# Two MLP layers planned task by task by the list scheduler, with the last attention pair's sums and products placed inside the first MLP

## The chip, the cores and the metric

The kernel runs on one core of one Trainium2 chip. The time is the device time of one execution in microseconds (us); the kernel before takes 679.59 us, the median of three runs (677.91, 679.59 and 680.23).

The core has a matrix engine (TensorE, PE in the rows), a vector engine (VectorE, DVE), a scalar engine (ScalarE, ACT), a general engine (GpSimd, called Pool here, POOL in the rows) and a queue that issues the loads and stores (SyncE, SP). Each engine does its own instructions in program order; between engines there are semaphores.

## The reference

Queries are averaged in twos, attention runs over 16 heads (2 batches of 8) of 1152 keys, and the 1152 x 512 result goes through two MLPs of 512 -> 2048 -> 512, the first with a leaky rectifier and the second with h times sigmoid(h). The weights arrive as 64-bit floats.

```python
def _attn_ref(q, k, v):                     # q, k, v: (2, 8, 1152, 64)
    q_pool = q.reshape(B, H, S // 2, 2, D).mean(axis=3)
    scores = scale * np.matmul(q_pool, k.transpose(0, 1, 3, 2))
    attn = np.exp(scores - np.max(scores, axis=-1, keepdims=True))
    attn = attn / (np.sum(attn, axis=-1, keepdims=True) + 1e-09)
    return np.matmul(attn, v)
...
x = attn_out.transpose(0, 2, 1, 3).reshape(B * S, H * D)     # 1152 x 512
h = x @ w_in;  x = np.maximum(0.01 * h, h) @ w_out           # first MLP
h = x @ w2_in; x = (h * (1.0 / (1.0 + np.exp(-h)))) @ w2_out # second MLP
```

## The kernel before

**Numbers in two parts.** TensorE multiplies operands of type fp32r. To keep precision every operand of the MLPs is held as a high part and a low part, and each product is three matmuls: high x high, low x high, high x low. So the MLPs' input is `xh` and `xl`, the weights are `w0h`/`w0l` (into the 2048) and `w1h`/`w1l` (out of them), and the values between are `gh` and `gl`.

**Attention.** Two heads make a pair; there are eight pairs. Their work is planned by `Plan`, a list scheduler that runs while the program is built: each task has an engine, an estimated length (`weight`), a due time, tasks that it comes after, and tokens or ring buffers that it takes and gives. Whenever an engine of the plan is free, the ready task with the earliest due time is written into the program. A pair's `pv` matmuls (L669) leave their sums in PSUM; ScalarE copies them to `pvs` (L683) in two halves. The sums of the exponentials come from `psum` matmuls with a tile of ones; for the last pair that is `sums_last`: TensorE L743 (two halves, two heads each), ScalarE L751 (to `r`), VectorE's reciprocals L757. Then `finish` multiplies (L766, VectorE), copies to `xh` (L769, ScalarE) and subtracts into `xl` (L770, VectorE). The last pair is the fourth 128-row slice of the second batch's columns, 576 to 1151.

**MLPs.** The 2048 inner columns are cut into four blocks of 512 (a block has four groups `f` of 128), the 1152 tokens into a narrow part of 512 and a wide part of 640 (two chunks of 320). A unit is (layer, block, part): 16 in all. `layer_in(u, f)` gives one PSUM tile `ph`: 12 matmuls of 512 columns, or 24 of 320. Then come the activation and the split: in the first MLP ScalarE twice (`gh`, `a`) and Pool `gl = a - gh` (L955); in the second ScalarE's sigmoid `t` (L952), VectorE's product `a` = h x t (L953), ScalarE's copy `gh` (L954), Pool's L955. `layer_out_t` (first MLP, `po`, L968) and `layer_out` (second, `pf`, L996) multiply the g tiles with the outgoing weights and add into an SBUF sum (L982 on VectorE). After the first MLP's last block ScalarE copies the sum to `xh` (L984) and Pool subtracts into `xl` (L985). `ph`, `po` and `pf` share four PSUM tiles; `t` and `a` have two buffers each.

**Weights.** They come in 64 pieces of 128 x 512 (four for each of a block's two matrices). A piece is loaded by SyncE (`raw`, three buffers), converted to 32 bits in five steps (ScalarE L131, then VectorE L135, L139, L143, L148, into `wt`, four buffers), and split (ScalarE L166 for the high part, Pool L170 for the low). Eight pieces are converted during attention, 56 in the MLPs.

**The order around the change.** Attention's plan ends before the MLPs begin. In `mlps` the order is written by hand: `phase_order` mixes the `layer_in` groups of a unit with the `layer_out` groups of the unit before, and at each `layer_in` group one piece is split, the next is converted with all its steps in one go, and one is loaded; only after that does `layer_in` write its own instructions (from the fourth unit on; the first two go by the tables `moe0` and `moe1`):

```python
        for x, u, i in order:
            if x is layer_in and ph > 2:
                weights.split()
                weights.convert()
                weights.load()
            x(u, i)
```

Of the kernel before, what the change touches and what calls it, by code (L numbers as in the profile page):

```python
# [19 lines left out]
def pooled_attention_two_mlps(  # L20
# [20 lines left out]
    with tc.manual_schedule():  # L41
        attention(tc, q, k, v, xh, xl, weights)
        mlps(tc, xh, xl, weights, out)
# [21 lines left out]
    weights_due=1.0,  # L65
    conv=8,
    split=4,
    wt=4,
    moe0=(0, 0, 0, 2),
    moe1=(2, 0, 1, 1),  # L70
# [216 lines left out]
def attention(ctx, tc, q, k, v, xh, xl, weights):  # L287
# [44 lines left out]
    ones = const.tile([128, D], F32, name="ones")  # L332
    tiny = const.tile([128, 1], F32, name="tiny")
# [317 lines left out]
    def sum_up(p, t, j, after, order, due):  # L651
        on_dve = (p, t, j) in dve_adds

        def go():
            e = nc.vector if on_dve else nc.gpsimd
            if t == 1:
                acc[p, j] = sm_p.tile([128, SQ], F32, tag="acc", name="acc", bufs=4)
            e.tensor_tensor(out=acc[p, j], in0=e_t[p, j, 0] if t == 1 else acc[p, j], in1=e_t[p, j, t], op=ALU.add)  # L658
# [18 lines left out]
    def evac_pv(p, after, due):  # L677
        made = []
        for c in range(2):
            def go(c=c):  # L680
                if c == 0:
                    pvs[p] = sm_p.tile([128, 2, C], F32, tag="pvs", name="pvs", bufs=1)
                nc.scalar.activation(out=pvs[p][:, c, :], in_=vps.pop((p, c))[:, 0:C], func=ACTF.Copy)  # L683
# [6 lines left out]
    def sums(p, after, due):  # L690
# [28 lines left out]
        def up2(j):  # L719
            if j == 0:  # L720
                rec[p] = sm_p.tile([128, 2, C], F32, tag="r", name="r", bufs=1)
# [15 lines left out]
    def sums_last(p, after, due):  # L737
        made = []
        for c in range(2):
            def pe(c=c):  # L740
                box["psum", c] = bank("psum")
                for j in range(2):
                    nc.tensor.matmul(  # L743
                        out=box["psum", c][0][own[j], 0:C], lhsT=ones, rhs=acc[p, j][:, c * C:(c + 1) * C], start=True, stop=True
                    )

            def act(c=c):
                ps, i = box.pop(("psum", c))
                if c == 0:
                    rec[p] = sm_p.tile([128, 2, C], F32, tag="r", name="r", bufs=1)  # L750
                nc.scalar.activation(out=rec[p][:, c, :], in_=ps[:, 0:C], func=ACTF.Identity, bias=tiny)  # L751
                banks.append(i)

            x = add("PE", 0.6, due, pe, after=after, take=("bank",))
            x = add("ACT", 0.5, due, act, after=[x], order=made, give=("bank",), take=() if c else ("r",))
            made.append(
                add("DVE", 1.95, due, lambda c=c: nc.vector.reciprocal(out=rec[p][:, c, :], in_=rec[p][:, c, :]), after=[x])  # L757
            )
        return made
# [36 lines left out]
    for p in range(NP):  # L796
# [62 lines left out]
        else:  # L859
            finish(p, sums_last(p, ends, at(1.0)) + values, at(1.0))  # L860
# [38 lines left out]
    attention.plan = plan  # L899
# [3 lines left out]
def mlps(ctx, tc, xh, xl, weights, out):  # L903
# [3 lines left out]
    FB, NBLK = weights.FB, weights.NBLK  # L907
    for key in ((0, 1), (1, 0), (1, 1)):
# [7 lines left out]


    groups = ((0, 1, 512), (512, 2, 320))
    g_t = {}
# [5 lines left out]
    def layer_in(u, f):  # L925
        layer, blk, g = u
        _, nch, n = groups[g]
        wh, wl = weights.tiles[layer * NBLK + blk, 0]
        fs = slice(f * 128, (f + 1) * 128)
        ps = ps_p.tile([128, 2, 512], F32, tag="p", name="ph")  # L930
        for kk in range(KDM):
            for wt, m in ((wh, xh), (wh, xl), (wl, xh)):
                for c in range(nch):
                    nc.tensor.matmul(  # L934
                        out=ps[:, c, 0:n],
                        lhsT=wt[:, kk, fs],
                        rhs=m[:, kk, chunk(g, c)],
                        start=(kk == 0 and wt is wh and m is xh),
                        stop=(kk == KDM - 1 and wt is wl),
                    )  # L940
        h = ps[:, 0:nch, 0:n]
        t = t_p.tile([128, 640], F32, tag="t", name="t")
        a = t_p.tile([128, 640], F32, tag="a", name="a")
        t, a = (x[:, 0:nch * n] for x in (t, a))
        t3, a3 = (x.rearrange("p (c n) -> p c n", n=n) for x in (t, a))
        gh, gl = (g_p.tile([128, 640], F32R, tag=f"g{part}{f}", name=f"g{part}") for part in "hl")
        if layer == 0:
            gh3 = gh[:, 0:nch * n].rearrange("p (c n) -> p c n", n=n)
            nc.scalar.activation(out=gh3, in_=h, func=ACTF.Prelu, alpha=0.01)
            nc.scalar.activation(out=a3, in_=h, func=ACTF.Prelu, alpha=0.01)  # L950
        else:
            nc.scalar.activation(out=t3, in_=h, func=ACTF.Sigmoid)  # L952
            nc.vector.tensor_tensor(out=a3, in0=h, in1=t3, op=ALU.mult)  # L953
            nc.scalar.activation(out=gh[:, 0:nch * n], in_=a, func=ACTF.Copy)  # L954
        nc.gpsimd.tensor_tensor(out=gl[:, 0:nch * n], in0=a, in1=gh[:, 0:nch * n], op=ALU.subtract)  # L955
        g_t[u, f] = (gh, gl)

    def layer_out_t(u, m):
        _, blk, g = u
        t0, nch, n = groups[g]  # L960
        oh, ol = weights.tiles[blk, 1]
        ms = slice(m * 128, (m + 1) * 128)
# [122 lines left out]
```

## Time and profile before

| | us |
|---|---|
| median of three runs | 679.59 |
| the profiled execution | 679.8 |
| its span, first to last instruction | 678.0 |
| TensorE busy (matmuls) | 654.2 (97%) |
| VectorE busy | 452.3 (67%) |
| Pool busy | 379.6 (56%) |
| ScalarE busy | 320.7 (47%) |
| moved by DMA | 59.71 MB, 88 GB/s on the mean |

An engine's busy time is the sum of its instructions' times in the profiled execution, and its share is taken of the span. Matmuls are pipelined, so that a busy share of TensorE near 100% does not tell how fast it goes: starts of instructions and the granted clock tell that. The DMA engines have little to do (their busy share is some 30% of the span).

### The profile page before, as it was taken

Reading aid. Unit: us, or ns where it says so; the run is one execution under the profiler, and the core shown is the slowest. Engines: PE = TensorE matmul, PEld = TensorE weight load, DVE = VectorE, ACT = ScalarE, POOL = GpSimd, SP = SyncE. Lnnn points to the kernel's source line nnn. Section 1 sums busy time; section 2 is a strip of 40 time slices with the busy share of each in tenths; the row PEclk is TensorE's granted clock in tenths of the full one; section 3 lists DMA queues with packets and bytes.
Section 4 is the critical chain, followed back from the end, with each engine's and each line's share of the span. In section 5 each row is a group of like instructions: output and inputs, shape, how many; then the busy total and the mean of one; then the engine's idle time right before and its main releaser. Section 6 shows DMA issues by size and latency. Waiting matters only on the chain.

```text
span 678.0 us, 10325 instructions
## 1 busy us (share of the span) xinstructions
PE 654.2 (97%) x3741; PEld 530.3 (78%) x3741; DVE 452.3 (67%) x698; ACT 320.7 (47%) x694; POOL 379.6 (56%) x294
## 2 busy tenths in 40 slices
PE   6899999999999999999999999999989999999997
PEld 4566667666666666989989989989867898888986
DVE  6776768587888867496667557476756677886222
ACT  5446566585766565555434234235344444334120
POOL 7566978878797830765445445365544354445120
PEclk9899999999999999999999999999989999999999
DMA  5535151536455220033223123012122222210012
GB/s 142 148 81 155 37 141 37 141 91 198 113 157 151 50 64 19 31 125 94 94 94 100 66 94 111 35 63 94 63 93 82 74 94 93 92 66 1 0 47 93
DMA packets 41898, 59.71 MB, mean 88 GB/s; under 512 B 15325, under 2 KB 24569, under 8 KB 41849
## 3 DMA queue, kind: packets, MB, share of 16 engines
q1 hardware_dynamic: 41848, 59.07, 29.9%
q8 instruction: 29, 0.48, 0.3%
q14 instruction: 21, 0.16, 0.1%
HBM read 49.81 MB, written 2.42 MB: 77 GB/s over the span
## 4 chain that ended last, share of the span: by engine, by line
PE 77%; DVE 12%; ACT 4%; DMA 3%; issue 2%; POOL 0%; SPq 0%; ACTq 0%; DVEq 0%
PE ph L934 24%; PE po L968 13%; PE pf L996 12%; PE pss L637 10%; PE pv L669 10%; PE pmx L583 4%; DVE mx L587 3%; PE prep L434 2%; DVE wt L139 2%; DVE wt L135 2%; DVE wt L143 1%; DMA d<-sum 1%; DVE a L953 1%; ACT wt L131 1%; DVE ql L491 1%
## 5 line engine op out<-in xcount | busy, mean ns | idle before, releaser
L955 POOL TENSOR_TENSOR gl<-a,gh 128x512 fp32r<-128x512 f32 (+1 forms) x64 | 95.1, 1488 | 163.4 <-ACT gh L954 107.5
L658 POOL TENSOR_TENSOR acc<-acc,e 128x576 f32<-128x576 f32 x98 | 140.1, 1451 | 29.0 <-ACT e L641 26.6
L641 ACT ACTIVATE e<-pss 128x288 f32<-128x288 f32 x288 | 101.4, 411 | 79.9 <-PE pss L637 73.0
L587 DVE TENSOR_REDUCE mx<-pmx 128x1 f32<-128x384 f32 x216 | 110.7, 550 | 34.4 <-PE pmx L583 29.2
L934 PE MATMUL ph<-xh,w0h 128*128 128x320 f32 (+1 forms) x384 | 109.1, 339 | 5.1 <-DVE a L953 4.5
L934 PE MATMUL ph<-xl,w0h 128*128 128x320 f32 (+1 forms) x384 | 108.9, 338 | 0.0
L934 PE MATMUL ph<-xh,w0l 128*128 128x320 f32 (+1 forms) x384 | 108.8, 338 | 0.0
L135 DVE TENSOR_SCALAR wt<-wt 128x512 f32<-128x512 f32 x56 | 44.6, 796 | 77.3 <-ACT wt L131 68.6
L637 PE MATMUL pss<-qh,k 128*128 128x288 f32 x288 | 87.8, 321 | 3.1 <-DVE mx L587 3.0
L669 PE MATMUL pv<-e,vnat 128*64 128x288 f32 x576 | 86.5, 422 | 0.0
L637 PE MATMUL pss<-ql,ka 128*128 128x288 f32 x288 | 81.2, 298 | 1.6 <-DMA ql<-mn 1.6
L934 PEld LDWEIGHTS ph<-xh,w0h 128*128 128x128 f32 x384 | 67.9, 189 | 13.1 <-DVE a L953 6.0
L637 PEld LDWEIGHTS pss<-qh,k 128*128 128x128 f32 x288 | 54.6, 190 | 24.9 <-DVE mx L587 10.3
L934 PEld LDWEIGHTS ph<-xh,w0l 128*128 128x128 f32 x384 | 67.5, 189 | 5.1
L934 PEld LDWEIGHTS ph<-xl,w0h 128*128 128x128 f32 x384 | 67.3, 189 | 4.6
L583 PE MATMUL pmx<-k,qh 128*128 128x384 f32 x192 | 65.4, 386 | 2.2 <-ACT e L641 1.0
L954 ACT ACTIVATE gh<-a 128x512 fp32r<-128x512 f32 (+1 forms) x32 | 22.0, 686 | 95.0 <-DVE a L953 95.0
L170 POOL TENSOR_TENSOR w1l<-wt,w1h 128x512 fp32r<-128x512 f32 x32 | 44.0, 1381 | 39.8 <-ACT w1h L166 39.8
L669 PEld LDWEIGHTS pv<-e,vnat 128*64 128x64 f32 x576 | 35.4, 137 | 28.9 <-issue 13.5
L996 PE MATMUL pf<-w1h,gh 128*128 128x512 f32 x144 | 56.5, 392 | 0.4 <-DVE a L953 0.3
L996 PE MATMUL pf<-w1h,gl 128*128 128x512 f32 x144 | 56.2, 390 | 0.6 <-POOL gl L955 0.6
L637 PEld LDWEIGHTS pss<-ql,ka 128*128 128x128 f32 x288 | 54.7, 190 | 2.0 <-issue 2.0
(82 smaller groups left out, 1137.7 us busy)
## 6 DMA issues: line engine op xcount, KB each, us to landing
wraw<-in_moe_w_in_dram SPq DMA_DIRECT2D x32, 512.0 KB, 3.8
wraw<-in_moe_w_out_dram SPq DMA_DIRECT2D x32, 512.0 KB, 3.3
vnat<-in_v_dram SPq DMA_DIRECT2D x8, 576.0 KB, 5.7
qnat<-in_q_dram SPq DMA_DIRECT2D x16, 256.0 KB, 4.7
knat<-in_k_dram SPq DMA_DIRECT2D x7, 576.0 KB, 5.4
ka<-k SPq DMA_DIRECT2D x16, 160.0 KB, 2.6
out_dram<-acc SPq DMA_DIRECT2D x9, 256.0 KB, 2.0
ka<-k SPq DMA_DIRECT2D x16, 128.0 KB, 2.5
```

The costliest lines, as they stand in the source:

```text
L135: nc.vector.tensor_scalar(out=tf, in0=tf, scalar1=2.0, scalar2=W_TOP, op0=ALU.max, op1=ALU.min)
L170: self.nc.gpsimd.tensor_tensor(out=lo, in0=tf, in1=hi, op=ALU.subtract)
L583: nc.tensor.matmul(out=ps[:, 0:KC], lhsT=QH[p, j][:, t * 128:(t + 1) * 128], rhs=K2[p, j][:, ks], start=True, stop=True)
L587: nc.vector.tensor_reduce(out=mx[p][:, n:n + 1], in_=ps[:, 0:KC], op=ALU.max, axis=AX.X)
L637: nc.tensor.matmul(out=ps[:, 0:C], lhsT=lhsT[:, ks], rhs=rhs[:, cs], start=not last, stop=last)
L641: nc.scalar.activation(out=e_t[p, j, t][:, cs], in_=ps[:, 0:C], func=ACTF.Exp, scale=scale)
L658: e.tensor_tensor(out=acc[p, j], in0=e_t[p, j, 0] if t == 1 else acc[p, j], in1=e_t[p, j, t], op=ALU.add)
L669: nc.tensor.matmul(out=vps[p, c][own[j], 0:C], lhsT=vnat[p][:, j, t, :], rhs=e_t[p, j, t][:, c * C:(c + 1) * C], start=(t == 0), stop=(t = ...
L934: nc.tensor.matmul(out=ps[:, c, 0:n], lhsT=wt[:, kk, fs], rhs=m[:, kk, chunk(g, c)], start=(kk == 0 and wt is wh and m is xh), stop=(kk == ...
L955: nc.gpsimd.tensor_tensor(out=gl[:, 0:nch * n], in0=a, in1=gh[:, 0:nch * n], op=ALU.subtract)
L968: nc.tensor.matmul(out=ps[:, c, 0:n], lhsT=wt[:, f, ms], rhs=x[:, c * n:(c + 1) * n], start=(f == 0 and wt is oh and x is gh), stop=(f == ...
L996: nc.tensor.matmul(out=ps[:, 0, :], lhsT=x[:, ts], rhs=wt[:, f, :], start=(f == 0 and x is gh and wt is oh), stop=(f == FB - 1 and x is gl),)
```

## The change

`sums_last` and its `finish` leave the attention's plan. A function `end` returns their steps instead: one step for TensorE (the four `psum` matmuls into one PSUM tile of the MLPs), one readout on ScalarE, and for each of two halves of 288 columns a reciprocal, a product, a copy to `xh` and a subtraction into `xl`. `pvs`, `r`, `acc`, `ones` and `tiny` move to a pool that lives through the MLPs.

`mlps` makes a `Plan` of its own. TensorE's groups get due times by adding up their estimated lengths in the order of `phase_order`, which is kept. Each group is four tasks (one for each `kk` or `f`), and each activation, product, copy, subtraction and sum is one task, due 3 us after its group's due time. A weight piece's load, five conversion steps and two split steps are tasks of their own, due `ahead` = 12 us before the piece's block is first used, plus 0.7 us for each piece in it. The pair's end is due at 2.5 us. Buffers are rings in the plan, as many as before. `moe0` and `moe1` go.

```diff
+    end=2.5,
+    ahead=12.0,
-    moe0=(0, 0, 0, 2),
-    moe1=(2, 0, 1, 1),
...
-    def sums_last(p, after, due):
+    def end(ps_p):
...
+        def pe():
+            box["end"] = ps_p.tile([128, 2, 512], F32, tag="p", name="psum")
+            for c in range(2):
                 for j in range(2):
...
+        def act():
+            rec[p] = end_p.tile([128, 2, C], F32, tag="r", name="r")
+            nc.scalar.activation(out=rec[p], in_=box["end"][:, :, 0:C], func=ACTF.Identity, bias=tiny)
...
-        else:
-            finish(p, sums_last(p, ends, at(1.0)) + values, at(1.0))
...
+    plan = Plan()
+    add = plan.add
+    for name, n in (("p", 4), ("t", 2), ("a", 2), ("raw", 3), ("wt", P["wt"])):
+        plan.ring(name, n)
+    for f in range(FB):
+        plan.ring(("g", f), 2)
...
+    for x in order:
+        kind, (layer, blk, g), i = x
+        due[x] = now
+        now += 3 * FB * (0.227 if g == 0 or (kind == "out" and layer == 1) else 0.292)
...
+    def piece_due(n):
+        blk, kind, i = pieces[n]
+        return first[blk, kind] - P["ahead"] + 0.7 * i
...
+                weigh = (("ACT", 0.66), ("DVE", 0.8), ("DVE", 1.1), ("DVE", 0.75), ("DVE", 0.75))
+                for m, (step, (eng, w)) in enumerate(zip(weights.convert_steps(), weigh)):
+                    x = [add(
+                        eng, w, d, step, after=x, order=[conv] if m == 0 and conv else [],
+                        take=(("wt", n),) if m == 0 else (), give=(("raw", n),) if m == 4 else (),
+                    )]
...
+            hi = add("ACT", 0.62, d, high, after=x, order=[hi] if hi else [])
+            lo = add("POOL", 1.45, d, low, after=[hi], give=(("wt", n),))
...
+            b = add(
+                "DVE", 0.83 if wide else 0.69, d,
+                lambda: nc.vector.tensor_tensor(out=three(tile("a")), in0=h(), in1=three(box["t", x]), op=ALU.mult),
+                after=[b], take=(("a", x),), give=(("p", x), ("t", x)),
+            )
...
+        t = add("PE", 1.2, P["end"], pe, take=(("p", "end"),), begin=P["end"])
+        t = add("ACT", 0.65, P["end"], act, after=[t], give=(("p", "end"),))
+        made = []
+        for c in range(2):
+            y = t
+            for m, (eng, w) in enumerate((("DVE", 1.93), ("DVE", 0.45), ("ACT", 0.45), ("DVE", 0.45))):
+                y = add(eng, w, P["end"], steps[c][m], after=[y])
```

Three places show what moves. A row here is one instruction in program order: line, operation, tile written <- tiles read, shape; the number behind a name tells its buffers apart, and the two programs number theirs differently.

The first is VectorE, and beside it ScalarE, early in the second MLP, at the second wide `ph` group of its first block, the one whose product is `a_5495` before and `a_5507` in the changed kernel. L953 and L1088 are the product. VectorE before:

```order
L135 TENSOR_SCALAR wt_5461<-wt_5461 128x512
L139 TENSOR_SCALAR wt_5461<-wt_5461 128x512
L143 SCALAR_TENSOR_TENSOR wt_5461<-wraw_5360,wt_5461 128x512
L148 SCALAR_TENSOR_TENSOR wt_5461<-wraw_5360,wt_5461 128x512
L953 TENSOR_TENSOR a_5495<-ph_5469,t_5494 128x640
L135 TENSOR_SCALAR wt_5518<-wt_5518 128x512
```

VectorE in the changed kernel:

```order
L135 TENSOR_SCALAR wt_5473<-wt_5473 128x512
L139 TENSOR_SCALAR wt_5473<-wt_5473 128x512
L143 SCALAR_TENSOR_TENSOR wt_5473<-wraw_5354,wt_5473 128x512
L1088 TENSOR_TENSOR a_5507<-ph_5453,t_5498 128x640
L148 SCALAR_TENSOR_TENSOR wt_5473<-wraw_5354,wt_5473 128x512
L135 TENSOR_SCALAR wt_5540<-wt_5540 128x512
L139 TENSOR_SCALAR wt_5540<-wt_5540 128x512
L1088 TENSOR_TENSOR a_5560<-ph_5516,t_5555 128x640
```

ScalarE before, at the same product (L952 sigmoid, L954 `gh`, L166 high part of a piece, L131 first step of the next):

```order
L954 ACTIVATE gh_5453<-a_5452 128x640
L166 ACTIVATE w0h_5383<-wt_5418 128x512
L131 ACTIVATE wt_5461<-wraw_5360 128x512
L952 ACTIVATE t_5494<-ph_5469 128x640
L954 ACTIVATE gh_5496<-a_5495 128x640
```

ScalarE in the changed kernel (L1084 sigmoid, L1093 `gh`):

```order
L131 ACTIVATE wt_5473<-wraw_5354 128x512
L1093 ACTIVATE gh_5482<-a_5471 128x640
L1084 ACTIVATE t_5498<-ph_5453 128x640
L1093 ACTIVATE gh_5513<-a_5507 128x640
L1179 ACTIVATE acc1_3466<-pf_5494 128x512
L166 ACTIVATE w1h_5408<-wt_5473 128x512
L131 ACTIVATE wt_5540<-wraw_5403 128x512
```

Before, each product follows a whole piece; in the changed kernel it follows three steps of one piece, and the next product the last step of it and two of the next. ScalarE's L131 for the piece ahead of this product stood behind the `gh` of the product before; in the changed kernel it stands ahead of that `gh`.

The second place is Pool where the first MLP's last wide unit turns into the second's input. Before, the four `xl` stand together:

```order
L170 TENSOR_TENSOR w1l_5135<-wt_5180,w1h_5134 128x512
L955 TENSOR_TENSOR gl_5235<-a_5233,gh_5234 128x512
L985 TENSOR_TENSOR xl_59<-acc1_3477,xh_58 128x640 x4
L170 TENSOR_TENSOR w1l_5135<-wt_5211,w1h_5134 128x512
L955 TENSOR_TENSOR gl_5378<-a_5376,gh_5377 128x512
```

In the changed kernel (L1149 is `xl`, L1099 `gl`):

```order
L1099 TENSOR_TENSOR gl_5248<-a_5238,gh_5247 128x512
L170 TENSOR_TENSOR w0l_5190<-wt_5196,w0h_5189 128x512
L1149 TENSOR_TENSOR xl_59<-acc1_3466,xh_58 128x640
L170 TENSOR_TENSOR w0l_5190<-wt_5250,w0h_5189 128x512
L1149 TENSOR_TENSOR xl_59<-acc1_3466,xh_58 128x640 x2
L170 TENSOR_TENSOR w0l_5190<-wt_5302,w0h_5189 128x512
L1149 TENSOR_TENSOR xl_59<-acc1_3466,xh_58 128x640
L170 TENSOR_TENSOR w1l_5409<-wt_5356,w1h_5408 128x512
```

Two weight splits stand among the four `xl` there. On VectorE the sums that they need (L1138 in the changed kernel) have conversion steps among them likewise, L148 and L135 ahead of the fourth.

The third place is TensorE where the MLPs begin. Before, the last pair's `psum` matmuls stand ahead of the first `ph` group:

```order
L743 MATMUL psum_3431<-acc_3238,ones_95 64x288
L743 MATMUL psum_3431<-acc_3248,ones_95 64x288
L743 MATMUL psum_3437<-acc_3238,ones_95 64x288
L743 MATMUL psum_3437<-acc_3248,ones_95 64x288
L934 MATMUL ph_3488<-xh_58,w0h_2050 128x512
```

In the changed kernel they stand behind the twelve matmuls of that group, of which the last three are shown:

```order
L1046 MATMUL ph_3467<-xh_58,w0h_2053 128x512
L1046 MATMUL ph_3467<-xl_59,w0h_2053 128x512
L1046 MATMUL ph_3467<-xh_58,w0l_2054 128x512
L747 MATMUL psum_3490<-acc_3241,ones_98 64x288
L747 MATMUL psum_3490<-acc_3251,ones_98 64x288
L747 MATMUL psum_3490<-acc_3241,ones_98 64x288
L747 MATMUL psum_3490<-acc_3251,ones_98 64x288
L1046 MATMUL ph_3502<-xh_58,w0h_2053 128x512
```

The second `ph` group follows them. Nothing else moves on TensorE, and nothing on SyncE's queue.

## Rows read from the trace of the kernel before

**Rows 1.** Windows view, us: PE, PEld, DVE, ACT, POOL busy (instructions), clock, DMA share, GB/s.

```profile
457.40:536.00 78.60, 72.71 (x374) 62.94 (x373) 51.31 (x65) 34.10 (x59) 37.88 (x27) 0.98 0.25 81
...
sum 407.90, PE 401.99 PEld 358.94 DVE 256.05 ACT 158.90 POOL 187.30; mean PE 134.00 PEld 119.65 DVE 85.35 ACT 52.97 POOL 62.43
```

**Rows 2.** Waits of TensorE, 263 to 680: us in total, times, longest.

```profile
PE ph L934 <- DVE a L953: 4.5, 3, 3.3
```

**Rows 3.** Timeline of TensorE: start, us, operation, [idle before <- what ended it].

```profile
457.46 0.45 PE L968 MATMUL po<-gh,w1h 128*128 128x320 f32 x2
...
498.54 0.56 PE L934 MATMUL ph<-xh,w0h 128*128 128x320 f32 x2 [3.28 <-DVE a L953]
...
499.23 0.73 PE L934 MATMUL ph<-xh,w0l 128*128 128x320 f32 x2
499.76 0.73 PE L934 MATMUL ph<-xh,w0h 128*128 128x320 f32 x2
...
535.98 0.56 PE L934 MATMUL ph<-xh,w0h 128*128 128x320 f32 x2 [0.36 <-DVE a L953]
```

**Rows 4.** Chain of work that ended last: start, us, what, matmuls.

```profile
259.64 1.12 PE pv L669 x8
...
585.75 7.09 PE ph L934 x48
...
618.99 2.72 PE ph L934 x12
...
635.31 10.55 PE ph L934 x72
...
648.61 3.52 PE ph L934 x24
```

**Rows 5.** Timeline of VectorE, in the MLPs.

```profile
265.42 3.77 DVE L757 RECIPROCAL r<-r 128x288 f32<-128x288 f32 x2 [1.32 <-ACT r L751]
...
454.68 0.43 DVE L139 TENSOR_SCALAR wt<-wt 128x512 uint32<-128x512 uint32 x1
...
468.38 2.27 DVE L982 TENSOR_TENSOR acc<-po,acc 128x640 f32<-128x640 f32 x3
...
494.05 0.83 DVE L135 TENSOR_SCALAR wt<-wt 128x512 f32<-128x512 f32 x1 [1.88 <-ACT wt L131]
494.91 1.38 DVE L139 TENSOR_SCALAR wt<-wt 128x512 uint32<-128x512 uint32 x1
...
497.66 0.82 DVE L953 TENSOR_TENSOR a<-ph,t 128x640 f32<-128x640 f32 x1
```

**Rows 6.** Timeline of ScalarE, at three places.

```profile
263.69 0.90 ACT L683 ACTIVATE pvs<-pv 128x288 f32<-128x288 f32 x2 [0.55 <-PE pv L669]
...
473.20 0.74 ACT L984 ACTIVATE xh<-acc 128x640 fp32r<-128x640 f32 x1 [1.77 <-DVE acc L982]
...
498.51 0.74 ACT L954 ACTIVATE gh<-a 128x640 fp32r<-128x640 f32 x1 [3.90 <-DVE a L953]
```

**Rows 7.** VectorE's groups by line, 263 to 680: count | busy us, mean ns | idle before.

```profile
L135 DVE TENSOR_SCALAR wt<-wt 128x512 f32<-128x512 f32 x56 | 44.6, 796 | 77.3 <-ACT wt L131 68.6 <-POOL gl L955 8.7
L139 DVE TENSOR_SCALAR wt<-wt 128x512 uint32<-128x512 uint32 x56 | 51.2, 914 | 1.9
L143 DVE SCALAR_TENSOR_TENSOR wt<-wraw,wt 128x512 uint32<-128x512 uint32 x56 | 48.3, 862 | 1.9
L148 DVE SCALAR_TENSOR_TENSOR wt<-wraw,wt 128x512 uint32<-128x512 uint32 x56 | 52.2, 932 | 1.9
```

**Rows 8.** Timeline of Pool.

```profile
469.21 1.31 POOL L955 TENSOR_TENSOR gl<-a,gh 128x512 fp32r<-128x512 f32 x1 [3.08 <-ACT gh L954]
470.46 6.19 POOL L985 TENSOR_TENSOR xl<-acc,xh 128x640 fp32r<-128x640 f32 x4
...
494.56 1.46 POOL L170 TENSOR_TENSOR w0l<-wt,w0h 128x512 fp32r<-128x512 f32 x1
```

**Rows 9.** Timeline of TensorE, start of the MLPs.

```profile
265.92 0.50 PE L934 MATMUL ph<-xh,w0h 128*128 128x512 f32 x1 [0.59 <-ACT r L751]
```

More of the change, by code (lines that the diff above doesn't have):

```diff
@@ L286, in attention @@
 @with_exitstack
-def attention(ctx, tc, q, k, v, xh, xl, weights):
+def attention(ctx, tc, q, k, v, xh, xl, weights, end_p):
     nc = tc.nc
@@ L898, in attention, with mlps @@
     plan.run()
-    attention.plan = plan
+    return end
 @with_exitstack
-def mlps(ctx, tc, xh, xl, weights, out):
+def mlps(ctx, tc, xh, xl, weights, out, end):
     nc = tc.nc
@@ L923, in chunk @@
         return slice(t0 + c * n, t0 + (c + 1) * n)
[L925 to L956, printed above, removed]
@@ L987, in layer_out, with columns @@
[L987 to L1009 removed]
+    def columns(g):
+        return groups[g][1] * groups[g][2]
@@ new lines, in mlps @@
+            outs = [("out", w, i) for i in range(KDM if w[0] == 0 else columns(w[2]) // 128)]
+        order += phase_order(ph, ins, outs)
+    due, now = {}, 0.0
+    for x in order:
+        kind, (layer, blk, g), i = x
+        due[x] = now
+        now += 3 * FB * (0.227 if g == 0 or (kind == "out" and layer == 1) else 0.292)
+    first = {}
+    for x in order:
+        kind, (layer, blk, g), i = x
+        first.setdefault((layer * NBLK + blk, int(kind == "out")), due[x])
+    pieces = weights.pieces
@@ new lines, in mlps, with split_of, matmuls @@
+    weight_tasks()
+    def split_of(blk, kind, i):
+        return split_t[pieces.index((blk, kind, i))]
+    def matmuls(x, tiles, deps, take):
+        kind, (layer, blk, g), i = x
+        w = 3 * (0.227 if g == 0 or (kind == "out" and layer == 1) else 0.292)
+        made = []
+        for k in range(FB):
+            t = add(
+                "PE", w, due[x], lambda k=k: tiles(k), after=deps(k), order=made[-1:], take=(take,) if k == 0 else (), lag=0.25
+            )
+            made.append(t)
+            users.setdefault((layer * NBLK + blk, int(kind == "out")), []).append(t)
+        return made
@@ new lines, in mlps @@
+    pair_end()
+    g_users = {}
+    for x in order:
+        kind, u, i = x
+        if kind == "in":
+            layer_in(x)
+        else:
+            g_users.setdefault(u, []).append((layer_out_t if u[0] == 0 else layer_out)(x))
+    for u, ts in g_users.items():
+        add("-", 0.0, 0.0, after=ts, give=tuple((("g", f), u) for f in range(FB)))
+    for hi, (blk, kind, i) in late:
+        if i == 0:
+            for t in users.get((blk - 2, kind), []):
+                plan.edge(t, hi)
```

294 lines of the change are left out of this document (193 added, 101 removed).

## The prediction

> **What bounds the kernel now.** I read the windows first. From 265.90 us to the last matmul at 673.80 us the kernel is in its two MLPs, and TensorE is the engine that sets the time: it is busy for 401.99 of 407.90 us, and nearly all that is missing (5.89 us) is missing in one stretch, 457.40 to 536.00, the change from the first MLP to the second, where the granted clock also averages 0.98 [rows 1]. Then the waits of TensorE: what they name most is the product `a` of VectorE, 4.5 us in three waits, the longest 3.3 us [rows 2]. A busy sum hides what pipelining and clock cost, so I size the loss from starts. From the start of the first MLP's last four `po` groups at 457.46 to 535.98, where the next block's wide `ph` groups begin, are 78.52 us [rows 3]. The program has 8 groups of 24 matmuls of 320 columns there and 15 groups of 12 of 512. An undisturbed group takes 3.52 and 2.72 us [rows 4], so 8 x 3.52 + 15 x 2.72 = 68.96 us; 9.56 us are lost. A block without a wait, 585.75 to 635.31, takes 49.56 us [rows 4] where its 4 and 13 groups give 49.44; that is 0.12 us in 50 that no order removes, 0.17 us in this stretch. **9.4 us can be won there**, and nothing elsewhere: outside this stretch TensorE is busy for 401.99 - 72.71 = 329.28 of 407.90 - 78.60 = 329.30 us [rows 1].
>
> Why TensorE waits is seen on VectorE, one turn before the longest wait: VectorE is idle for 1.88 us until ScalarE's copy L131 is there, then does the four conversion steps of a weight piece, and only then, at 497.66, the product [rows 5]. ScalarE's `gh` had waited 3.90 us for this product [rows 6], and behind `gh`, in ScalarE's order, stand the split L166, the next L131 and the next sigmoid. So one piece and one product form a loop: from 492.17, where VectorE falls idle, to the product's end at 498.48 are 6.3 us a turn, most of it serial. TensorE needs a product every 4.5 us here: from the third group of the first unit to the second of the next are 4 x 3.52 + 4 x 2.72 for eight `ph` groups and 4 x 2.72 for the four `pf` between them, 35.8 us for eight. The loop falls behind, four PSUM tiles are used up, and TensorE stops. After the longest stop (3.28 us) pairs of matmuls start 0.53 us apart [rows 3] instead of 3.52 / 12 = 0.29 us: that is the 1.2 GHz level of the clock.
>
> **The change, part by part.** *The list scheduler in the MLPs.* TensorE's groups keep their order, SP's queue reads the same, and no arithmetic is added except a split into halves for the last pair. What moves are ScalarE's, VectorE's and Pool's rows. In the built order the product no longer stands behind four steps of a piece but behind one to three, and ScalarE's L131 no longer stands right behind the `gh` of the product before. The loop is then cut, and what is left is VectorE's own work: a piece costs 0.796 + 0.914 + 0.862 + 0.932 = 3.50 us [rows 7] and a product 0.82 us [rows 5], 4.3 us a turn against the 4.5 us that TensorE takes. Four PSUM tiles cover single late products. So I count the stretch as nearly free of waits: **-9.4 us**, the clock's part with it, since it follows a stop.
>
> What may stay is bounded from both sides. The lower end is 0 us. The upper end is one stop as long as the longest now, 3.3 us [rows 2]. The two tight places that I worked through: (1) the second MLP's input of the wide unit. In the changed order Pool's four subtractions `xl` have two weight splits among them, and VectorE's sum for the fourth row block stands behind the steps L148 and L135. Without a queue the way from its last matmul to `xl` is a sum of 2.27 / 3 = 0.76 us [rows 5], a copy of 0.74 us [rows 6] and a subtraction of 6.19 / 4 = 1.55 us [rows 8], 3.05 us. TensorE comes to it two `ph` groups of 2.72 us, three quarters of a wide group and one pair later: 5.44 + 2.64 + 0.29 = 8.4 us. That leaves 5.3 us for the queues: two steps at their mean (0.93 + 0.80), one split and one L131 on ScalarE (about 1.3 us, two copies of this size), one split on Pool (1.46 us [rows 8]), 4.5 us: no wait. If both steps meet a Pool split, each is held up to 0.95 us more, as L139 is (1.38 us against 0.43 [rows 5]): 6.4 us, a wait of 1.1 us. (2) The product of the second wide group, ahead of the group that stops for 3.28 us now: three steps of one piece stand before it, 2.57 us at their means against 3.50 us and an idle 1.88 us now. I take **+0.5 us** for both, nearer to zero because at mean durations neither waits.
>
> A step's duration hangs on Pool. L139 takes 0.43 us at 454.68, but 1.38 us at 494.91 [rows 5], where it ends 0.27 us after a Pool split that had begun at 494.56 and ended at 496.02 [rows 8]. Three sums that read PSUM took 0.76 us each from 468.38 on [rows 5], although Pool was busy from 469.21 [rows 8]. The Trainium skill, SBUF — State Buffer, section Who interferes with whom, states this as an exclusive lock: of Pool and a VectorE instruction with two SBUF inputs or in a two-port mode the one that issues second blocks until the first has ended, and a VectorE instruction with at most one SBUF input does not contend. The rows agree. By that rule the product, which reads one PSUM and one SBUF tile, is late only by the step in progress, and the sum stays; if the product were held up as L139 is, about 1 us more for each would make the turn 5.3 us, which is the first rival below. In the other direction the rule speaks against the change, because interleaving gives each step a Pool instruction of its own to meet: that is the last rival.
>
> *The last pair's end.* Now TensorE does the pair's sums (`psum`) first and starts the MLP at 265.92, when ScalarE has read them out [rows 9]. In the changed order the first `ph` group stands ahead of `psum` and waits for the second copy of `pvs`, because of its PSUM bank. That copy ends at 263.69 + 0.90 = 264.59 [rows 6], and the MLP starts there at the earliest. But `psum` is moved, not removed: eight passes of this shape take 1.12 us in the chain of work [rows 4], and they now stand inside the MLP. 265.92 - 264.59 - 1.12 = 0.21: **-0.2 us**. What hides the rest of the pair's end: sums out at 264.6 + 2.72 + 1.12 = 268.4, a readout behind two copies of `gh` and `a` until about 269.5, two reciprocals (3.77 us together, as they are now [rows 5]) until 273.3, and the second half's product, copy and subtraction, half a us to one us each, until about 275.5. The first wide group needs the last of them at 264.6 + 1.12 + 4 x 2.72 + 2.64 = 279.2. The cover is 3.7 us, and the one conversion step among them costs 0.86 us of it, up to 0.95 more if it meets Pool. Without cover each us would count in full; I take 0, with ends 0 and 1.
>
> *Weights.* Pieces are made 12 us ahead of the first use instead of one for each `ph` group. No wait for a weight is among TensorE's now. In the built order each piece's halves stand well ahead of the group that reads them, and the loads' rows are the same; I take 0.
>
> *Sum.* 678.0 - 9.4 + 0.5 - 0.2 = 668.9 us of span. The profiled execution took 679.8 us, 1.8 us more than its span, so 670.7 us; it lies 0.2 us above the median of the three runs shown, 679.59. Forecast: **670.5 us**.
>
> **The rivals.** *A part of the stops stays.* For it: VectorE's turn of 4.3 us is close to TensorE's 4.5, and Pool decides it. If two steps of each piece meet a Pool instruction, a turn is 5.3 us, 0.8 us over, 6.6 us in eight turns; PSUM tiles in hand take off some 2 us: 4.6 us stay, 675 us. Against it: the 3.50 us are means in which such meetings are already counted. *Nothing to be seen.* The loop would only be moved, to the earlier blocks, where conversions now compete with the first MLP's `gl`: TensorE's loss would stay near 9 us and the time at 679. Against it: outside the stretch VectorE is busy for 256.05 - 51.31 = 204.74 of 329.30 us and Pool for 149.42 [rows 1], and TensorE has no wait there; VectorE has 124 us to spare. *Slower.* VectorE becomes the bound of the MLPs. Of its 256.05 us [rows 1] 196.3 are the 56 pieces' steps [rows 7]; 59.8 us are other work. If the scheduler's mixing lets nearly every step meet a Pool instruction, a piece grows; at (407.9 - 59.8) / 56 = 6.2 us VectorE needs as long as the MLPs take now, and from there on the kernel is slower: at 6.5 us a piece VectorE needs 424 us, and the time is 679.6 + 16 = 696 us. Against it: that is nearly twice today's mean, and Pool is busy for less than half of the MLPs.
>
> **How the numbers follow.** The forecast with residual waits of 0 to 3 us (668.8 to 673.0 us) gets 0.79, a part of the stops (673 to 677.5) 0.12, nothing to be seen 0.05, slower 0.04. A measurement of this kernel can tell about 0.3%, 2 us, from no change. Faster by more than that: 0.79 + 0.12 = 0.91; within it 0.05; slower 0.04. The lower end of the range is the sum without the residual (670.0) less 1.2 us, since the runs shown lie from 677.91 to 680.23. The upper end goes a third into the first rival, 674.5, which leaves out some 0.15 in all.
>
> **What would show it.** Right: TensorE without a wait over 0.5 us between 457 and 536 us, the stretch at about 69 us, clock 1.00 in it, the product behind at most three steps; the MLP's first matmul at 264.6 and `psum` 2.7 us later. Wrong: waits for `xl` at the first wide group of the second MLP or for `a` at the third or fourth; VectorE's L135 to L148 at more than 3.7 us a piece; waits on weights, on `gl` or on the pair's `xl`, which TensorE does not have now.

## The result: 1.0% faster, the stops at the change of layers gone

The changed kernel takes 673.36 us (median of seven runs, 670.57 to 676.84) against 680.12 us for the kernel before on the same chips (677.91 to 684.34). The ratio is 0.990 (95% interval 0.988 to 0.992): faster by 6.7 us, where the forecast of 670.5 from 679.59 was 9.1 us. The time lies inside the stated range. By the prediction's own bands, though, 673.36 us belongs not to the forecast (668.8 to 673.0) but to the first rival (673 to 677.5), whose stops did not occur: the time alone would have named the wrong mechanism.

Executions of one and the same kernel differ by up to 6.4 us (677.91 to 684.34). In the twelve profiles of this study, one for each kernel, the MLPs' first matmul starts between 265.0 and 270.9 us, with attention's program nearly the same in all, so that much of the difference can come from ahead of the MLPs. What a change does to the MLPs is therefore read from their own length, from the start of the first `ph` matmul to the start of the last matmul plus 0.23 us: 407.83 us before, 401.27 us in the changed kernel.

All the waits of TensorE that end in the MLPs, changed kernel (us in total, times, longest), which answers to [rows 2]:

```profile
PE ph L1046 <- ACT pvs L684: 0.5, 1, 0.5
```

One wait is left, at the very start. The timeline of TensorE shows that start, the pair's sums inside the MLP, and the two ends of the stretch of [rows 3]:

```profile
265.12 0.50 PE L1046 MATMUL ph<-xh,w0h 128*128 128x512 f32 x1 [0.54 <-ACT pvs L684]
...
268.07 1.19 PE L747 MATMUL psum<-acc,ones 128*64 128x288 f32 x8
...
458.72 0.46 PE L1117 MATMUL po<-gh,w1h 128*128 128x320 f32 x2
...
528.21 0.46 PE L1046 MATMUL ph<-xh,w0h 128*128 128x320 f32 x2
```

The windows view cut at that stretch (us; busy of PE, PEld, DVE, ACT, POOL with instructions; clock, DMA share, GB/s), to be held against [rows 1]:

```profile
458.70:528.20 69.50, 69.50 (x373) 61.94 (x372) 61.43 (x71) 35.53 (x61) 41.34 (x28) 1.00 0.30 98
```

The stretch that took 78.52 us takes 528.21 - 458.72 = 69.49 us, at a granted clock of 1.00: 9.03 us won there. The MLPs as a whole won only 407.83 - 401.27 = 6.56 us. Of the difference of 2.47 us, 1.12 are the `psum` matmuls, which moved in from outside; 1.35 us have to be found.

VectorE around the product of the second wide group, changed kernel, which answers to [rows 5]:

```profile
488.37 1.06 DVE L135 TENSOR_SCALAR wt<-wt 128x512 f32<-128x512 f32 x1 [0.53 <-ACT wt L131]
489.46 1.69 DVE L139 TENSOR_SCALAR wt<-wt 128x512 uint32<-128x512 uint32 x1
491.18 0.69 DVE L143 SCALAR_TENSOR_TENSOR wt<-wraw,wt 128x512 uint32<-128x512 uint32 x1
491.79 0.82 DVE L1088 TENSOR_TENSOR a<-ph,t 128x640 f32<-128x640 f32 x1
```

Three steps stand ahead of this product, and VectorE waited 0.53 us for L131 where it was 1.88 us. It is not so for all: in the same timeline the ten products from 481.25 to 522.86 have 3, 2, 2, 3, 3, 5, 7, 2, 4 and 4 steps between themselves and the product or sum before.

And VectorE's pieces in the MLPs by line (count | busy us, mean ns | idle before and what ended it), against [rows 7]:

```profile
L139 DVE TENSOR_SCALAR wt<-wt 128x512 uint32<-128x512 uint32 x56 | 57.9, 1033 | 1.7
L143 DVE SCALAR_TENSOR_TENSOR wt<-wraw,wt 128x512 uint32<-128x512 uint32 x56 | 51.9, 927 | 1.2
L148 DVE SCALAR_TENSOR_TENSOR wt<-wraw,wt 128x512 uint32<-128x512 uint32 x56 | 51.7, 924 | 1.7
L135 DVE TENSOR_SCALAR wt<-wt 128x512 f32<-128x512 f32 x56 | 40.4, 722 | 49.6 <-ACT wt L131 49.6
```

A piece takes 3.61 us (3.50 before), and the idle time that ends with L131 fell from 68.6 to 49.6 us.

### The profile page after: what moved, and what is told of

Read it like the earlier page. It is cut to its first block, busy times and chain, and to the rows that moved or that the text cites. A ratio compares the mean times of both kernels' runs of the same rounds, so it can differ in the third digit from the quotient of the medians.

```text
span 670.6 us, 10322 instructions
## 1 busy us (share of the span) xinstructions
PE 653.0 (97%) x3741; PEld 530.1 (79%) x3741; DVE 456.1 (68%) x700; ACT 322.7 (48%) x694; POOL 385.3 (57%) x294
## 4 chain that ended last, share of the span: by engine, by line
PE 87%; DVE 6%; DMA 3%; ACT 1%; issue 1%; SPq 1%; POOL 0%; DVEq 0%; ACTq 0%
PE ph L1046 30%; PE po L1117 15%; PE pf L1166 15%; PE pss L638 10%; PE pv L670 10%; PE pmx L584 4%; DVE mx L588 3%; PE prep L435 2%; DMA d<-sum 1%; DVE ql L492 1%; DMA r<-d 1%; DMA cmp<-d 1%; DMA qnat<-in_q_dram 1%; ACT qh L352 1%; SPq L347 1%
## 5 line engine op out<-in xcount | busy, mean ns | idle before, releaser
L1099 POOL TENSOR_TENSOR gl<-a,gh 128x512 fp32r<-128x512 f32 (+1 forms) x64 | 97.2, 1519 | 142.7 <-ACT gh L1093 76.1
L135 DVE TENSOR_SCALAR wt<-wt 128x512 f32<-128x512 f32 x56 | 40.4, 722 | 49.6 <-ACT wt L131 49.6
L139 DVE TENSOR_SCALAR wt<-wt 128x512 uint32<-128x512 uint32 x56 | 57.9, 1033 | 1.7
L170 POOL TENSOR_TENSOR w0l<-wt,w0h 128x512 fp32r<-128x512 f32 x32 | 44.7, 1397 | 24.7 <-ACT w0h L166 24.7
L1166 PE MATMUL pf<-w1l,gh 128*128 128x512 f32 x144 | 56.1, 390 | 0.0
```

The costliest lines, as they stand in the source:

```text
L139: nc.vector.tensor_scalar(out=t, in0=t, scalar1=4, scalar2=1, op0=ALU.logical_shift_left, op1=ALU.logical_shift_right)
L170: self.nc.gpsimd.tensor_tensor(out=lo, in0=tf, in1=hi, op=ALU.subtract)
L1099: nc.gpsimd.tensor_tensor(out=gl, in0=box["a", x], in1=gh, op=ALU.subtract)
L1166: nc.tensor.matmul(out=box[x][:, 0, :], lhsT=y[:, ts], rhs=wt[:, f, :], start=(f == 0 and y is gh and wt is oh), stop=(f == FB - 1 and y i ...
```

## The experiments

All ratios are to the kernel before, timed on the same chip; MLP length and the mean start-to-start time of 512-column matmuls within a group are read from TensorE's timeline of one execution of each kernel. Only those marked * have the 1.12 us of `psum` in the length.

| kernel | ratio (95%) | median, us | MLPs, us | 512 columns, us |
|---|---|---|---|---|
| before | 1 | 680.12 | 407.83 | 0.2277 |
| changed * | 0.990 (0.988, 0.992) | 673.36 | 401.27 | 0.2289 |
| plan alone | 0.988 (0.986, 0.990) | 673.50 | 399.88 | 0.2288 |
| copy early | 0.988 (0.985, 0.991) | 673.24 | 398.18 | 0.2274 |
| product between | 0.987 (0.984, 0.990) | 672.80 | 399.04 | 0.2274 |
| piece in one * | 0.991 (0.987, 0.994) | 676.10 | 405.01 | 0.2288 |
| 32 bytes, changed kernel * | 0.989 (0.986, 0.991) | 672.49 | 401.20 | 0.2292 |
| 32 bytes, kernel before | 1.003 (1.001, 1.004) | 682.35 | 409.00 | 0.2288 |
| product between, three tiles | one run | 676.38 | 404.46 | 0.2274 |
| copy early, three tiles | one run | 674.91 | 401.22 | 0.2274 |
| same place * | 0.987 (0.984, 0.990) | 671.51 | 399.56 | 0.2277 |
| `gl` twice * | one run | 695.10 | 423.64 | 0.2291 |

### Which half of the change: the plan alone

```diff
+        else:
+            finish(p, sums_last(p, ends, at(1.0)) + values, at(1.0))
...
-    pair_end()
```

> The changed kernel with the last pair's sums and products back in the attention's plan; only the MLPs' plan is left of the change. Theory (the plan carries the gain, the pair's end is moved work): first matmul of the MLPs 0.5 to 1.3 us later than in the changed kernel, 1.12 us of psum less inside the MLPs, so the time within 0.5 us of the changed kernel, 6 to 7 us below the kernel before. Rival (the pair's end carries part of it): 1 us or more slower than the changed kernel.

673.50 us, the changed kernel's time to 0.14 us; the ratios, 0.988 and 0.990, have overlapping intervals, so that the times cannot tell the two apart. The chain of work at the start of the MLPs (start, us, what), with the plan alone and then in the changed kernel:

```profile
263.71 2.09 PE pv L670 x16
265.81 0.76 PE psum L774 x4
...
267.63 18.21 PE ph L1072 x96
```

```profile
262.50 2.14 PE pv L670 x16
...
265.12 3.01 PE ph L1046 x12
268.14 1.12 PE psum L747 x8
```

From the end of the last `pv` to the first `ph` are 267.63 - 265.80 = 1.83 us with the plan alone, and 265.12 - 264.64 = 0.48 us in the changed kernel, which pays 1.12 us for `psum` later. In these two executions, then, the pair's end, moved, is worth 1.83 - 0.48 - 1.12 = 0.2 us, as forecast, and the plan carries the gain.

### Which edge of the loop: ScalarE's copy early, or the product between the steps

Two edits of the kernel before, each in the second MLP's `layer_in` only. The first leaves a product and the four steps of a piece taking turns on VectorE and puts L131 ahead of `gh`, with the split behind it (`layer_in` issues the steps that it is handed right behind the sigmoid; each product moves ahead of the piece that was converted just before it); the second leaves ScalarE's order and puts the product between the second and the third VectorE step.

```diff
+                x(u, i, steps[0:1])
+                weights.split()
+                for step in steps[1:]:
+                    step()
```

> The kernel before, in the second MLP only one thing moved: ScalarE's copy L131 of a piece stands ahead of the gh of the same group and the split L166 behind it; VectorE still does a product and then four steps in a row. Theory (the loop through ScalarE: gh 0.74, split 0.61, L131 0.57, then the steps and the product, a turn of some 6 us against TensorE's 4.5): VectorE's turn is 4.3 us, the wait for L131 is gone, the stretch of 78.5 us comes to 69 to 71 us and the time falls by 7 to 9 us. Rival (the product's place behind a whole piece on VectorE is what counts): stretch 77 to 79 us, time as before.

```diff
+                weights.split()
...
+                for step in steps[0:3]:
+                    step()
+                x(u, i)
+                for step in steps[3:]:
+                    step()
```

> The kernel before, in the second MLP only VectorE's order changed: the product stands between the second and the third step of a piece, ScalarE's order as before. Theory (loop through ScalarE): the split still waits for the piece's last step and L131 for the split, so a turn is some 1.6 (two steps) + 0.61 + 0.57 + 2.0 (two steps) + 0.7 = 5.5 us in place of 5.8: 8 turns, 2 to 3 us won, time 677 to 678. Rival (the place behind a whole piece is what counts): 7 to 9 us won, as with the plan.

Both win all of it: the stretch takes 69.04 us with the copy early and 69.91 with the product between, and the kernels are as fast as the changed one. VectorE over one turn with the copy early:

```profile
490.02 0.81 DVE L955 TENSOR_TENSOR a<-ph,t 128x640 f32<-128x640 f32 x1
490.75 0.41 DVE L135 TENSOR_SCALAR wt<-wt 128x512 f32<-128x512 f32 x1
491.20 0.43 DVE L139 TENSOR_SCALAR wt<-wt 128x512 uint32<-128x512 uint32 x1
491.66 0.69 DVE L143 SCALAR_TENSOR_TENSOR wt<-wraw,wt 128x512 uint32<-128x512 uint32 x1
492.39 1.96 DVE L148 SCALAR_TENSOR_TENSOR wt<-wraw,wt 128x512 uint32<-128x512 uint32 x1
494.26 0.81 DVE L955 TENSOR_TENSOR a<-ph,t 128x640 f32<-128x640 f32 x1
```

and with the product between:

```profile
493.73 0.81 DVE L953 TENSOR_TENSOR a<-ph,t 128x640 f32<-128x640 f32 x1
494.46 0.67 DVE L143 SCALAR_TENSOR_TENSOR wt<-wraw,wt 128x512 uint32<-128x512 uint32 x1
495.17 0.69 DVE L148 SCALAR_TENSOR_TENSOR wt<-wraw,wt 128x512 uint32<-128x512 uint32 x1
497.12 0.46 DVE L135 TENSOR_SCALAR wt<-wt 128x512 f32<-128x512 f32 x1 [1.26 <-ACT wt L131]
497.62 1.40 DVE L139 TENSOR_SCALAR wt<-wt 128x512 uint32<-128x512 uint32 x1
498.94 0.81 DVE L953 TENSOR_TENSOR a<-ph,t 128x640 f32<-128x640 f32 x1
```

With the copy early VectorE is never idle in the turn, and a whole piece still stands ahead of each product: the rival theory, that the product's place behind a whole piece decides, falls. (The head start of one piece is not the reason: the ninth product, at 510.59, starts 0.9 us after TensorE has ended its group, with only the sigmoid between, so VectorE keeps up.)

With the product between, VectorE still waits 1.26 us for L131 in nearly every turn, and a turn is 498.94 - 493.73 = 5.21 us, close to the 5.5 expected. But TensorE waits for a product once, for 0.6 us, where only 2 to 3 of the 9.4 us were expected to be won. The loop theory has the turn right and the price wrong. The mean turn does not give the price: ten products from 478.37 to 524.86 are nine turns of 5.17 us, but TensorE itself takes 44.9 us for these nine, 5.0 each, since `pf` groups stand between the last of them. What counts is how late one product is, that of the second wide group. TensorE, in its timeline, ends that group's matmuls at 484.83, where the next row begins, and the fourth wide group waits for the product:

```profile
484.83 0.39 PE L996 MATMUL pf<-w1h,gh 128*128 128x512 f32 x1
...
494.60 0.56 PE L934 MATMUL ph<-xh,w0h 128*128 128x320 f32 x2 [0.60 <-DVE a L953]
```

The product starts at 493.73, 8.9 us behind its group. In the kernel before it was 13.0 us (484.65 to 497.66); it is 6.5 in the changed kernel (485.32 to 491.79) and 5.3 with the copy early (489.00 to 494.26). Where nothing stops TensorE, the fourth wide group starts 9.0 us after the second has ended, with a `ph` and two `pf` between them. The product takes 0.81 us, so it may start up to 8.2 us behind its group before TensorE stops.

### What absorbs it: three PSUM tiles in place of four

```diff
-    ps_p = ctx.enter_context(tc.tile_pool(name="ps_p", bufs=4, space=PSUM))
+    ps_p = ctx.enter_context(tc.tile_pool(name="ps_p", bufs=3, space=PSUM))
```

> The product between the steps (turn of 5.2 us on VectorE against TensorE's 4.5, next to no wait) with three PSUM tiles in place of four. Theory (the tiles hold some 5 us of lag, one tile 3 us of it): the lag of some 0.65 us in each of eight turns no longer fits, TensorE waits 2 us or more for a in the change of layers, and the clock falls behind it: stretch 72 to 76 us. Rival (5.2 us a turn are enough without slack): waits under 1 us, stretch 69 to 70.

> ScalarE's copy early (turn of 4.8 us on VectorE, which is never idle in it) with three PSUM tiles. Theory: a lag of 0.3 us in each of eight turns, 2.4 us, just about fits: waits of 0 to 1.5 us for a, less than in the run with the product between the steps. Rival (three tiles are too few by themselves, whatever the turn): waits as long as there.

TensorE's waits in the MLPs, those for `a` with the product between and three tiles, and under it the two longest with the copy early and three tiles:

```profile
PE po L968 <- DVE a L953: 2.0, 2, 1.3
PE pf L996 <- DVE a L953: 1.4, 1, 1.4
...
PE ph L934 <- DVE a L953: 0.7, 1, 0.7
```

```profile
PE ph L934 <- ACT acc L982: 0.9, 1, 0.9
PE ph L934 <- DVE acc L1009: 0.7, 2, 0.4
```

VectorE's turns are the same 5.2 us with three tiles (490.33, 495.54, 500.76 in its timeline), yet TensorE now waits 4.1 us for `a`, the stretch takes 74.2 us, as expected, and the MLPs are 404.46 - 399.04 = 5.4 us longer. The granted clock of the stretch stays at 1.00 here, where the expectation had it fall. With the copy early there is no wait for `a`, as expected, and the stretch takes 69.5 us, though the MLPs are 3.0 us longer, with 1.8 us of waits for sums. So it is the fourth tile that lets a turn of 5.2 us pass. With three, the second `pf` behind the second wide group takes its tile again, 6.3 us after the group's end where nothing stops TensorE, and the second row above is that `pf` waiting 1.4 us for `a`; the product may then be 5.4 us late in place of 8.2. The copy early, with 5.3 us, just fits; the product between, with 7.9, does not. The 13.0 us of the kernel before fit neither.

### Do the steps have to be mixed: a piece in one task

```diff
-                    x = [add(
-                        eng, w, d, step, after=x, order=[conv] if m == 0 and conv else [],
...
+                begin, *rest = weights.convert_steps()
+                x = [add("ACT", 0.66, d, begin, after=x, order=[conv] if conv else [], take=(("wt", n),))]
+                x = [add("DVE", 3.4, d, lambda rest=rest: [step() for step in rest], after=x, give=(("raw", n),))]
```

> The changed kernel, but the four VectorE steps of a piece are one task of the plan, so that no product or sum comes between them. Theory (the gain comes from L131 made ahead, not from interleaving): TensorE waits under 1 us in all, time within 1 us of the changed kernel. Rival (the interleaving is what counts): most of the 9 us in the stretch come back, time 678 to 680.

The median of 676.1 us is neither number, but the ratio, 0.991 (0.987 to 0.994), cannot be told from the changed kernel's 0.990. The profiled execution shows more: its MLPs are 3.7 us longer than in the changed kernel, and the wait is not for the product. The longest wait of TensorE, then its timeline behind it, then Pool ahead of it:

```profile
PE ph L1043 <- POOL xl L1146: 1.9, 1, 1.9
```

```profile
483.24 0.56 PE L1043 MATMUL ph<-xl,w0h 128*128 128x320 f32 x2 [1.92 <-POOL xl L1146]
...
484.57 0.73 PE L1043 MATMUL ph<-xl,w0h 128*128 128x320 f32 x2
485.11 0.73 PE L1043 MATMUL ph<-xh,w0l 128*128 128x320 f32 x2
```

```profile
477.26 4.25 POOL L170 TENSOR_TENSOR w1l<-wt,w1h 128x512 fp32r<-128x512 f32 x3
481.48 1.71 POOL L1146 TENSOR_TENSOR xl<-acc,xh 128x640 fp32r<-128x640 f32 x1
```

It is the tight place (1) of the prediction. Without the mixing, three splits stand together on Pool ahead of the fourth `xl`, and TensorE stops for 1.92 us. Behind the stop, pairs of matmuls start 0.54 us apart in place of 0.29, with a granted clock of 0.50 from 484.2 to 487: the 1.2 GHz level costs about as much again as the stop (3.7 us in all). For the product, L131 made ahead is enough; in the plan's order the mixing is needed for the second MLP's input. The copy early and the product between, ordered by hand, need none there: their Pool does the four `xl` in a row.

### Where 1.35 us went: the place of the tiles in SBUF

In the table the first three kernels with the plan (changed, plan alone, piece in one) have their 512-column matmuls 0.2288 us apart, those ordered by hand (before, copy early, product between) 0.2275; 950 such intervals make 1.2 us. The chain of work shows it best at the first two `ph` groups of the second block, in the changed kernel and, below it, in the kernel before:

```profile
302.73 5.60 PE ph L1046 x24
```

```profile
302.12 5.44 PE ph L934 x24
```

The last pair's tiles, which now live through the MLPs, take 14,112 bytes of each partition ahead of `w1`, the odd blocks' `w0`, the g tiles and the sums.

```diff
+    ctx.enter_context(tc.tile_pool(name="pad", bufs=1)).tile([128, 8], F32, name="pad")
     for key in ((0, 1), (1, 0), (1, 1)):
```

> The changed kernel with 32 unused bytes in each SBUF partition ahead of the MLPs' pools, so that w1, the odd blocks' w0, gh, gl, t, a and the sums start at multiples of 64 bytes again, as in the kernel before (the last pair's tiles, 14,112 bytes, had moved them by 32). Theory (the address costs the 512-column groups their 0.5%): matmuls of 512 columns start 0.2275 us apart in place of 0.2289, the odd blocks' ph 0.227 in place of 0.233; 953 of them, so the MLPs take 1.3 us less: 400.0 in place of 401.3 us from the first matmul to the last. Rival (it is the plan's order, or chance): 0.2289 and 401.3 as before.

> The kernel before with the same 32 bytes, which here move the same tiles off the multiples of 64; order and everything else unchanged. Theory (the address): 512-column matmuls 0.2288 us apart in place of 0.2277, odd blocks' ph 0.233, and 1 to 1.5 us more in the MLPs. Rival (the order): 0.2277 as before.

The 32 bytes did nothing for the changed kernel, and gave the kernel before the plan's 0.2288, with the same order of instructions. So the order is not the cause, and multiples of 64 are not the condition (14,112 + 32 = 14,144 is one). With `[128, 568]` in place of `[128, 8]`:

> The changed kernel with 2,272 unused bytes in each SBUF partition ahead of the MLPs' pools. In the kernel before w0, w1, xh, xl and acc1 all start at 128 above a multiple of 1,024 bytes; the last pair's tiles moved the odd blocks' w0 and what follows off it, and multiples of 64 did not bring the spacing back. With the 2,272 bytes all of them start at 128 above a multiple of 1,024 again. Theory (the place relative to the others costs it): matmuls of 512 columns 0.2276 us apart in place of 0.2289, odd blocks' ph 0.227 in place of 0.233, MLPs 400.0 us in place of 401.3. Rival (the plan's order, since a shift by 32 alone gave the kernel before the same 0.2288 by chance): 0.2289.

The same two groups in the changed kernel with 32 bytes, in the kernel before with 32 bytes, and with the tiles at the same place (three kernels, chain of work):

```profile
303.40 5.60 PE ph L1047 x24
```

```profile
303.46 5.60 PE ph L935 x24
```

```profile
303.28 5.44 PE ph L1047 x24
```

0.2277 us, 399.56 us for the MLPs: 1.7 us came back. That is more than the 1.35 us looked for, because the place also costs inside the stretch of [rows 3], which takes 69.04 us here in place of 69.49. The median, 671.51 us, is the lowest of the study, but the ratio, 0.987, is that of the product between. That the place causes it is shown: 14,112 + 2,272 = 16,384 bytes bring the spacing back, 14,144 do not. Which operand it is, and which multiple counts, stays open.

### The price of the slower rival: `gl` twice

```diff
+            for _ in range(2):
                 nc.gpsimd.tensor_tensor(out=gl, in0=box["a", x], in1=gh, op=ALU.subtract)
```

> The changed kernel with each gl computed twice on Pool (the second time over the first, the same result): 97 us of Pool work more in the MLPs, its busy share from 48 to 72%. A piece's four steps take 3.61 us now, and 2.21 where Pool holds none of them up, so 1.4 us are Pool's doing at 48%. Theory (VectorE has room for that): a piece at 72% takes 2.21 + 2.1 = 4.3 us, VectorE is busy for some 300 of 402 us, and what TensorE waits for, if anything, is gl itself, since Pool then needs 2 x 1.6 + 1.4 = 4.6 us for a wide group and its piece against TensorE's 4.5: 0 to 6 us more. Rival (VectorE becomes the bound, at 6.2 us a piece): 15 us or more, and the waits are for a, for weights and for the sums.

695.1 us. The windows view of the MLPs (columns as above), VectorE's pieces and products by line, and the longest of TensorE's waits:

```profile
266.00:690.00 424.00, 408.73 (x2168) 357.98 (x2166) 330.59 (x313) 158.98 (x273) 302.16 (x196) 1.00 0.22 71
```

```profile
L148 DVE SCALAR_TENSOR_TENSOR wt<-wraw,wt 128x512 uint32<-128x512 uint32 x56 | 82.3, 1470 | 1.7
L143 DVE SCALAR_TENSOR_TENSOR wt<-wraw,wt 128x512 uint32<-128x512 uint32 x56 | 77.8, 1389 | 1.2
L139 DVE TENSOR_SCALAR wt<-wt 128x512 uint32<-128x512 uint32 x56 | 55.9, 999 | 1.6
L135 DVE TENSOR_SCALAR wt<-wt 128x512 f32<-128x512 f32 x56 | 55.9, 998 | 28.9 <-ACT wt L131 28.9
...
L1088 DVE TENSOR_TENSOR a<-ph,t 128x640 f32<-128x640 f32 x16 | 13.1, 820 | 20.6 <-ACT t L1084 19.3 <-POOL gl L1100 1.2
```

```profile
PE ph L1046 <- POOL xl L1150: 3.2, 3, 1.5
PE po L1118 <- DVE acc L1139: 3.0, 4, 0.9
PE ph L1046 <- DVE acc L1139: 2.1, 3, 0.9
PE pf L1167 <- POOL gl L1100: 1.9, 1, 1.9
```

The MLPs take 423.64 us, 22.4 us more than in the changed kernel: the size is the rival's (15 us or more), the mechanism is neither theory's. A piece takes 1.470 + 1.389 + 0.999 + 0.998 = 4.86 us, more than the 4.3 expected and less than the rival's 6.2. Where Pool holds none of them up the four steps take 2.21 us (the rows further up have 0.41, 0.43, 0.69 and 0.69), so Pool, busy for 71% of the time, holds them up 2.65 us a piece, against 1.40 us at 48%: in the same order of instructions the hold-up grows faster than Pool's share. The share alone does not set it: with Pool at 49 and 50% it is 1.17 us in the product between (a piece of 3.38 us) and 1.62 in the copy early (3.83). VectorE is busy for 330.59 of 424.00 us and not the bound by its sum. TensorE's waits come to 14.3 us, many short ones: 7.3 for VectorE's sums and products, but 6.1 for Pool's own `xl` and `gl`, which the edit makes late by itself, so that the price of VectorE's slower pieces is not told apart. What makes up the rest of the 22.4 us is not shown beyond a granted clock of 0.96 from 440 to 480 us. The product still takes 0.82 us. The Trainium skill, SBUF — State Buffer, section Who interferes with whom, says that a VectorE instruction with at most one SBUF input, outside the two-port modes, does not contend with GpSimd; the product agrees, with Pool at 71% too.

## Why the prediction was right, and where its steps were off

**The stretch.** -9.4 + 0.5 = -8.9 us was forecast, 9.03 us were measured. TensorE waits for nothing there and the clock is 1.00. Right, but that the number is met so closely is partly luck: the 0.5 us of waits did not come, and the place of the tiles, which the prediction did not have, cost 0.45 us there. With the place restored 78.52 - 69.04 = 9.48 us are won.

**The reason: half right.** The loop through ScalarE and VectorE was the cause: cutting it by hand at ScalarE's copy, or shortening it at the product, wins the same. But the product is not "behind one to three" steps: up to seven stand ahead of it in the stretch, and TensorE does not wait, as it does not in the copy early, where a whole piece does. By the means of the lines a turn is 3.61 + 0.82 = 4.43 us, near the 4.3 forecast. It cannot be read from the products' starts: from 481.25 to 522.86 the changed kernel's ten products are 4.62 us apart, and TensorE itself ends their groups only every 4.94 us. Nor did so short a turn matter: 5.2 us in the product between cost one stop of 0.6 us. What lets it pass is the four PSUM tiles. The prediction had them take off "some 2 us" of a lag. Counted in its way, the product between lags 8 x (5.2 - 4.5) = 5.6 us, and 0.6 stopped TensorE: some 5 us were taken off (an estimate). That term was mis-sized, and with it the first rival: a turn of 5.3 us, priced at 4.6 us of stops, costs next to nothing. Nor does the rival's condition give its 5.3 us: one hold-up of 0.95 us on top of 4.3 does, two make 6.2.

**The tight places.** At mean durations neither was to wait, and neither does. That (1) is tight is shown by the piece in one task, where just this place stops for 1.92 us. In the changed kernel the last `xl` ends at 480.78, 0.4 us before TensorE reads it at 481.2.

**The pair's end.** -0.2 us forecast, 0.2 us won. The pair's last `xl` was put at 275.5 and came at 276.79, after one conversion step in between; it was needed at 279.3. The cover held, with 2.5 us where 3.7 were reckoned.

**Weights at nothing, and nothing else.** No wait for a weight. But the step "what moves are ScalarE's, VectorE's and Pool's rows" left out what the diff also moves: the place of the tiles in SBUF. It cost 1.35 us of the MLPs outside the stretch and 0.45 inside, and 1.7 us came back with the place restored. This is the step that failed, in the time as well.

**The sum.** Span 668.9 forecast, 670.6 measured: 0.1 us less in the stretch, 1.35 more for the place of the tiles, 0.5 more because attention's last copies ended at 265.08 in this execution, not at 264.59. The profiled execution took 2.8 us more than its span, the other six runs 1.7 to 1.8; that microsecond is unexplained.

**The rivals.** Nothing to be seen: no. Slower: no, a piece grew from 3.50 to 3.61 us only. Its point of decision, 6.2 us a piece from VectorE's sum, was too generous: with a piece of 4.86 us, and Pool's own rows late as well, the MLPs are already 22 us longer, by waits that come long before VectorE's sum is full.

## What to carry to other kernels

Where two engines hand work to each other in a ring, write down for the latest hand-over how far it lags behind the bound engine, and when that engine needs the buffer again. Here any cut that brought the lag under that time won all of it, and a finer one no more. Under it a cheap hand edit (here, one copy ahead of one other instruction) can do as well as a planner. When a change makes tiles live longer, compare the addresses of all tiles behind them too.

## What was not expected of the hardware

With the same instructions in the same order, 32 bytes more ahead of the tiles make 512-column matmuls start 0.2288 us apart in place of 0.2277, in the odd blocks' `ph` groups 5.60 us in place of 5.44 for 24. In the changed kernel, whose tiles stand 14,112 bytes further on, the same went away with 16,384 bytes and not with 14,144. And in one order of instructions VectorE's steps slow more than in proportion to Pool: 1.40 us a piece at 48% of Pool's time, 2.65 us at 71%.
